# Mamba-2 scan and hard-swish MLP on one core: chunk 1's scan begun earlier within block 0's second product, weight parts cut into tiles of their own, and C and B of later chunks turned within the first product

## The chip, the cores and the metric

The kernel runs on one core of a Trainium2 chip. The metric is the device time of one execution in microseconds (us). Before the change, three runs gave 363.67, 364.67 and 365.08 us; their median, 364.67 us, is the time to compare with. The engines are named as in the profile: PE (matmuls), DVE (vector engine), ACT (scalar engine), POOL (GpSimd), SP (the queue that issues most DMAs).

## The reference, cut to what matters

```python
# scan: x (4, 8, 768, 32), a (4, 8, 768), B and C (4, 8, 768, 16)
for c in range(nc):
    cum = np.cumsum(la, axis=-1)                                   # la = log a of the chunk
    M = np.einsum('bhin,bhjn->bhij', Cc, Bc) * exp(cum_i - cum_j) * causal
    y = M @ xc + np.einsum('bhin,bhnd->bhid', Cc, state) * exp(cum)
    state = exp(sum la) * state + sum_j exp(cum_end - cum_j) * Bc_j xc_j
# (batch, head, seq, 32) -> 3072 rows of 256
h = x @ w_in                                                       # 256 x 2048
g = h * np.clip(h + 3.0, 0.0, 6.0) / 6.0
out = g @ w_out                                                    # 2048 x 256
```

## The kernel before, in words

**Blocks.** The 768 positions are cut into 6 chunks of 128. Chunk c gives, over 4 batches, 512 rows of 256 features, and these are block c of the MLP. Block k is computed in two products: the first (x @ w_in, with the hard-swish) in 16 units f of 128 features each, and the second (g @ w_out). The scan of chunk c = k + 1 runs within block k's second product, and its decays are loaded and made one chunk further ahead (`ahead` = k + 2).

**The scan of a chunk.** `turn` (or `turn_all`) turns B and C: bT, cT and csT, the last multiplied by the decay from the start, eto. `wake` makes the exponent of eto (ACT), `carry` (tmp, POOL) and `ends` (bs, POOL). `scores` is PE work: the old state into y (L501), the scores cb (L528), the new state's sums (L540). `multiply` multiplies the decays L by cb on DVE (L569), after `take`, a copy (adds) on ACT; `renew` makes the next state on DVE. `results` is `mix` (PE, L595 and L501), `keep` (four copies into yT on ACT, L610) and `split_y`, which cuts yT into three parts yh, yk and yl, so that the first product can run in a faster number type. `conceal` (POOL, L159) hides the upper triangle of the decays of the chunk ahead, and `decay_ends` makes their exponents, 8 on ACT (L386) and one product on POOL (L397) for each of 4 batches.

**The weights' parts.** In block 0 the first product uses w_in as it is. For the blocks after it, `in_weight_parts(i)`, i = 0 to 3, makes of each quarter of w_in the cut wh (ACT, L666, written over w_in itself), the remainder wl (POOL, L658) and a third part wk (DVE, L661). Before, two cuts of 128x512 (DVE, L640) go through a tile with two buffers, and the pieces of the four quarters are issued one after the other at units 1 to 8 of block 0's second product (`first_out`, 16 units of 8 PE entries).

**The first product of blocks 1 to 5.** `first(k, f + 2)` (yk by wk), `rest(k, f)` (yh by wh and yl by wl), then `seed` (scales what `first` made, in PSUM; before on ACT for odd f (L702) and on DVE for even f (L704)), `ramp` (ACT, L718) and `times_ramp` (DVE, L723; its output is gT(f)). rest(f) needs seed(f), which was issued two units before. `lead` issues `first` and `seed` of units 0 and 1 near the end of the block before. After every fourth unit `g_sums` puts three sums of 128x512 on POOL (L785).

**The second product of blocks 1 to 4** is `wide_units` (PE, L872), in 15 steps i; the scan's parts are called at given i. It needs four sums of parts of w_out, made on DVE by `weight_sums` (L764).

**What sets the order.** All engines run their instructions in the order in which the program issues them, and this is written out by hand in the loops at the end. An instruction that waits holds up all that stands behind it on its engine.

Of the kernel before, what the change touches and what calls it, by code (L numbers as in the profile page):

```python
# [8 lines left out]
FP32 = mybir.dt.float32  # L9
FP32R = mybir.dt.float32r  # L10
U32 = mybir.dt.uint32
# [10 lines left out]
def kernel(  # L22
# [427 lines left out]
    def turn(c, j):  # L450
        if j:
            turn_b(c)
        else:
            t_ps = turn_ps(c, 0)
            turn_c(c, t_ps)
            fade_c(c, t_ps)

    def wake(c):
        from_start(c)
        carry(c)  # L460
        for b in range(NB):
            ends(c, b)

    def turn_squares(t, out):

        nc.vector.transpose(
            out=out.rearrange("r b (s a) -> r b a s", a=4),
            in_=t.rearrange("s t b a n -> s (b a) t n"))

    def part_heads(c):  # L470
        _, cT, csT = turned(c)
        for t in range(2):
            nc.vector.tensor_scalar(
                out=cT[:, :, t], in0=csT, scalar1=parity[:, t:t + 1], scalar2=None,
                op0=ALU.mult)

    def fade(c, sl=slice(0, P), engine=nc.vector):
        csT = turned(c)[2][:, :, sl]
        engine.tensor_tensor(out=csT, in0=csT, in1=etos[c][:, :, sl], op=ALU.mult)

    def turn_all(c):
        bT, _, csT = turned(c)
        for t, out_ in zip(bcs[c], (csT, bT)):
            turn_squares(t, out_)
        part_heads(c)
        fade(c)

    def busy(n, bank):

# [144 lines left out]
    cuts, y_parts, banks = {}, {}, {}  # L634
    wl, wk, wh = {}, {}, {}

    def cut(src):

        t = att.tile([P, TB], U32, name="cut")
        nc.vector.tensor_scalar(  # L640
            out=t, in0=src.bitcast(U32), scalar1=0xFFFFF000, scalar2=None, op0=ALU.bitwise_and)
        return t.bitcast(FP32)

    def in_weight_parts(i):

        w = w_in[i]
        if i < 2:
            l, k = (const.tile([P, NK, TB], FP32R, name=f"w{n}{i}") for n in "lk")
        elif i == 2:
            both = loads.tile([P, 2, NK, TB], FP32R, name="wlk", tag="raw", bufs=NRAW)  # L650
            l, k = both[:, 0], both[:, 1]
        else:
            l, k = ([att.tile([P, TB], FP32R, name=n, tag=n) for _ in range(NK)]
                    for n in ("ws", "we"))
        wl[i], wk[i] = ([t[:, j] if i < 3 else t[j] for j in range(NK)] for t in (l, k))
        cuts[i] = [cut(w[:, j]) for j in range(NK)]
        for j in range(NK):
            nc.gpsimd.tensor_tensor(out=wl[i][j], in0=w[:, j], in1=cuts[i][j], op=ALU.subtract)  # L658
        yield
        for j in range(NK):  # L660
            nc.vector.scalar_tensor_tensor(  # L661
                out=wk[i][j], in0=wl[i][j].bitcast(FP32), scalar=-1.0 / FINE, in1=cuts[i][j],
                op0=ALU.mult, op1=ALU.add)
        h = const.tile([P, NK, TB], FP32R, name="wh", tag=f"w{i}")
        for j in range(NK):
            nc.scalar.copy(out=h[:, j], in_=cuts[i][j])  # L666
        wh[i] = [h[:, j] for j in range(NK)]
        yield

    def split_y(k):  # L670
        h, l, m = (att.tile([P, NK, TB], FP32R, name=f"y{n}", bufs=1) for n in "hlk")
        y_parts[k] = h, l, m
        for j in range(NK):
            y = yTs[k][:, j].rearrange("p b i -> p (b i)")
            t = cut(y)
            nc.scalar.copy(out=h[:, j], in_=t)
            nc.vector.scalar_tensor_tensor(  # L677
                out=m[:, j], in0=t, scalar=1.0 + FINE, in1=y, op0=ALU.mult, op1=ALU.subtract)
            nc.vector.scalar_tensor_tensor(
                out=l[:, j], in0=m[:, j].bitcast(FP32), scalar=-1.0 / FINE, in1=t,  # L680
                op0=ALU.mult, op1=ALU.add)

    def product(k, f, w, y, start=False):
        for j in range(NK):
# [13 lines left out]

    def seed(k, f):
        h = banks[k, f]  # L700
        if f % 2:
            nc.scalar.activation(h, h, AF.Copy, scale=-1.0 / (1.0 + FINE))  # L702
        else:
            nc.vector.tensor_scalar(  # L704
                out=h, in0=h, scalar1=-1.0 / (1.0 + FINE), scalar2=None, op0=ALU.mult)
# [240 lines left out]
        load_decay(c)  # L946
        load_eto(c)

    def results(c, parts=range(2)):
        mix(c, parts)  # L950
        keep(c)
        split_y(c)

# [75 lines left out]
    for k in range(NC):  # L1029
        gTs[k] = ffn.tile([P, NF, TB], FP32, name="gT")  # L1030
        c, ahead = k + 1, k + 2
        if k == 0:
            for f in range(NF):
                mlp_in(k, f)
                for i in weave.get(f, []):
                    weights(i, 1)
                if f in (6, 8):
                    diff_exp(c, f // 2 - 3)
            load(ahead)
            weights(NP + 1, 1)  # L1040
            weights(NP + 3, 1)
            weights(NP + 2, 3)
            sums = weight_sums()
            parts_in = [in_weight_parts(i) for i in range(NP)]
            for i in range(NP):
                for b in range(NB):
                    first_out(b, i, c)
                    if (i, b) == (0, 0):
                        weights(NP + 3, 1)
                        weights(NP + 2, 1)  # L1050
                        weights(NP + 3, 3)
                        rows(ahead)
                    elif 4 * i + b < 9:
                        next(parts_in[(4 * i + b - 1) // 2])
                    if (i, b) == (2, 0):
                        turn(c, 1)
                        wake(c)
                        turn(c, 0)
                        for p in range(2):
                            conceal(ahead, p)  # L1060
                    elif (i, b) == (2, 3):
                        scores(c)
                        multiply(c)
                        renew(c)
                        decay_ends(ahead, 0)
                        decay_ends(ahead, 1)
                        next(sums)
                    elif (i, b) == (3, 0):
                        next(sums)
                        decay_ends(ahead, 2)  # L1070
                    elif (i, b) == (3, 1):
                        results(c)
                        next(sums)
                        decay_ends(ahead, 3)
                    elif (i, b) == (3, 3):
                        from_start(ahead)
            rows(ahead + 1)
            continue
        for f in range(NF):
            if f == 0:  # L1080
                if ahead < NC:
                    load(ahead)
                if c < NC:
                    carry(c)
            if f + 2 < NF:
                first(k, f + 2)
            rest(k, f)
            if f + 2 < NF:
                seed(k, f + 2)
            ramp(k, f, banks[k, f])  # L1090
            times_ramp(k, f, banks[k, f])
            if f in (3, 7) and ahead < NC:
                conceal(ahead, f // 4)
            if f in (7, 11) and c < TURN:
                turn(c, f // 8)
            if f % 4 == 3:
                g_sums(k, f // 2 - 1)
        for i, _ in enumerate((wide_units if c < NC else out_units)(k)):
            if i == 0 and k == 1:
                next(sums)  # L1100
            if c < NC:
                if i == 1 and c == NC - 1:
                    own_banks(c)
                if i == 2:
                    scores(c)
                    multiply(c)
                    if c < NC - 1:
                        renew(c)
                if ahead < NC and 2 <= i < 6:
                    decay_ends(ahead, i - 2)  # L1110
                if i == 6 and c == TURN:
                    mix(c, (0,))
                if i == (7 if c == TURN else 6):
                    results(c, (1,) if c == TURN else range(2))
                    if ahead < NC:
                        from_start(ahead)
                    if ahead + 1 < NC:
                        rows(ahead + 1)
                if i == 9 and TURN <= ahead < NC:
                    turn_all(ahead)  # L1120
                if i == 5:
                    for j0 in range(0, NJ, 2):
                        last_sum(k, j0)
                if i == 12:
                    lead(c)

# [29 lines left out]
```

## Time and profile before

| What | Value |
|---|---|
| Median of 3 runs | 364.67 us (363.67 to 365.08) |
| The profiled execution | 363.47 us, its span 361.7 us |
| PE busy | 334.8 us, 93% of the span |
| DVE, ACT, POOL busy | 228.4 us (63%), 179.0 us (49%), 148.6 us (41%) |
| PE's share in the chain that ended last | 68% |

The span runs from the first to the last instruction of the profiled execution; 1.8 us of its time lie outside it. A row of the timeline gives start and duration in us, the engine, the line, what is written from what, the shapes, the number of instructions, and in brackets the idle time of the engine before them with what ended it. Where several instructions share a row, the duration is that of all of them. In block 0 the second product's matmuls run on plain fp32 and each shows as two PE entries. The first products lie at about 102 to 124, 154 to 176, 207 to 228, 258 to 280 and 312 to 333 us.

### The profile page before, as it was taken

Reading aid. Unit: us, or ns where it says so; the run is one execution under the profiler, and the core shown is the slowest. Engines: PE = TensorE matmul, PEld = TensorE weight load, DVE = VectorE, ACT = ScalarE, POOL = GpSimd, SP = SyncE. Lnnn points to the kernel's source line nnn. Section 1 sums busy time; section 2 is a strip of 40 time slices with the busy share of each in tenths; the row PEclk is TensorE's granted clock in tenths of the full one; section 3 lists DMA queues with packets and bytes.
Section 4 is the critical chain, followed back from the end, with each engine's and each line's share of the span. In section 5 each row is a group of like instructions: output and inputs, shape, how many; then the busy total and the mean of one; then the engine's idle time right before and its main releaser. Section 6 shows DMA issues by size and latency. Waiting matters only on the chain.

```text
span 361.7 us, 8315 instructions
## 1 busy us (share of the span) xinstructions
PE 334.8 (93%) x3408; PEld 268.1 (74%) x3408; DVE 228.4 (63%) x364; ACT 179.0 (49%) x372; POOL 148.6 (41%) x147
## 2 busy tenths in 40 slices
PE   6699999906899999999999999999999989999996
PEld 2454468805677888878888788888888868888996
DVE  6689999774768743976444967348876413576011
ACT  4677886134876646256374166293267012266000
POOL 3300000557118956419816338716048450069600
PEclk9999999965999999999999999999999999999999
DMA  8999989400057603425604325600110001110000
GB/s 164 187 304 163 230 206 139 96 0 2 31 143 85 94 5 73 90 31 60 97 4 98 69 35 65 88 4 2 30 30 2 2 2 16 24 22 1 2 29 29
DMA packets 91606, 24.90 MB, mean 69 GB/s; under 512 B 84208, under 2 KB 87952, under 8 KB 91056
## 3 DMA queue, kind: packets, MB, share of 16 engines
q1 hardware_dynamic: 87184, 23.06, 34.9%
q10 hardware_dynamic: 4384, 1.31, 1.7%
q8 instruction: 26, 0.43, 0.5%
q14 instruction: 12, 0.10, 0.1%
HBM read 21.07 MB, written 3.29 MB: 67 GB/s over the span
## 4 chain that ended last, share of the span: by engine, by line
PE 68%; DVE 15%; ACT 6%; DMA 4%; POOL 3%; issue 3%; SPq 1%; DVEq 0%; POOLq 0%; ACTq 0%
PE h L685 29%; PE wb L872 10%; PE wc L872 7%; PE wa L872 7%; PE oa L808 3%; PE ob L808 3%; DVE gT L723 2%; PE cb L528 2%; PE y L595 2%; DVE wm L206 2%; PE y L501 2%; DMA eto<-cum_e 2%; DMA raw<-in_moe_w_in_dram 2%; ACT L L386 2%; ACT we L222 2%
## 5 line engine op out<-in xcount | busy, mean ns | idle before, releaser
L718 ACT ACTIVATE gT<-h,half 128x512 f32<-128x512 f32 x96 | 65.9, 687 | 45.4 <-PE h L685 43.5
L723 DVE SCALAR_TENSOR_TENSOR gT<-gT,h 128x512 f32<-128x512 f32 x96 | 65.8, 687 | 33.8 <-ACT gT L718 32.6
L785 POOL TENSOR_TENSOR s<-gT 128x512 f32<-128x512 f32 x20 | 26.7, 1336 | 66.6 <-DVE gT L723 66.6
L685 PE MATMUL h<-yh,wh 128*128 128x512 f32 x160 | 50.3, 396 | 1.2 <-DVE h L704 1.2
L685 PEld LDWEIGHTS h<-yh,wh 128*128 128x128 f32 x160 | 29.6, 188 | 9.6 <-DVE h L704 2.3
L702 ACT ACTIVATE h<-h 128x512 f32<-128x512 f32 x40 | 23.5, 587 | 19.4 <-PE h L685 19.4
L386 ACT ACTIVATE L<-L,cum_n 128x64 f32<-128x64 f32 x128 | 31.4, 338 | 0.0
L569 DVE TENSOR_TENSOR L<-L,cb 128x512 f32<-128x512 f32 x24 | 15.3, 682 | 21.8 <-PE cb L528 18.2
L737 PE MATMUL o<-w_out,gT 128*128 128x256 f32 x128 | 28.8, 381 | 0.0
L704 DVE TENSOR_SCALAR h<-h 128x512 f32<-128x512 f32 x40 | 27.5, 689 | 0.6 <-PE h L685 0.6
L620 PE MATMUL h<-yT,w_in 128*128 128x512 f32 x64 | 27.7, 594 | 0.0
L685 PE MATMUL h<-yk,wk 128*128 128x512 f32 x80 | 26.2, 416 | 1.4 <-DVE yk L677 1.4
L737 PEld LDWEIGHTS o<-w_out,gT 128*128 128x128 f32 x128 | 24.2, 191 | 3.9 <-issue 0.6
L397 POOL TENSOR_TENSOR bs<-B,L 128x128 f32<-128x128 f32 x24 | 9.7, 413 | 41.4 <-ACT L L386 30.5
L785 POOL TENSOR_TENSOR s<-s,gT 128x512 f32<-128x512 f32 x20 | 25.7, 1287 | 1.6
L658 POOL TENSOR_TENSOR wl<-w_in,cut 128x512 fp32r<-128x512 f32 x4 | 5.2, 1324 | 50.1 <-DVE cut L640 50.1
L785 POOL TENSOR_TENSOR gT<-gT 128x512 f32<-128x512 f32 x20 | 25.7, 1283 | 0.0
L685 PE MATMUL h<-yl,wl 128*128 128x512 f32 x80 | 25.0, 394 | 0.0
L792 POOL TENSOR_TENSOR gT<-gT,s 128x512 f32<-128x512 f32 x16 | 21.2, 1359 | 5.0 <-PE wc L872 5.0
L620 PEld LDWEIGHTS h<-yT,w_in 128*128 128x128 f32 x64 | 12.1, 190 | 14.9 <-issue 12.9
L159 POOL TENSOR_SCALAR_AFFINE_SELECT L<-L 64x1024 f32<-64x1024 f32 (+1 forms) x16 | 18.3, 1146 | 7.9 <-DMA L<-cum_d 7.5
L685 PEld LDWEIGHTS h<-yk,wk 128*128 128x128 f32 x80 | 15.0, 188 | 5.2 <-DVE yk L677 1.5
(156 smaller groups left out, 635.1 us busy)
## 6 DMA issues: line engine op xcount, KB each, us to landing
raw<-in_moe_w_out_dram SPq DMA_DIRECT2D x4, 1024.0 KB
L<-cum_d SPq DMA_DIRECT2D x8, 512.0 KB
xt<-in_x_dram SPq DMA_DIRECT2D x6, 512.0 KB
raw<-in_moe_w_in_dram SPq DMA_DIRECT2D x3, 1024.0 KB
out_dram<-back SPq DMA_DIRECT2D x128, 16.0 KB
eto<-cum_e SPq DMA_DIRECT2D x20, 64.0 KB
B<-in_B_dram SPq DMA_DIRECT2D x5, 256.0 KB
raw<-in_moe_w_in_dram ACTq DMA_DIRECT2D x1, 1024.0 KB
```

The source lines that it names most:

```text
L386: nc.scalar.activation(Ls[c][:, b, h], Ls[c][:, b, h], AF.Exp, bias=cum_n[:, c, g:g + 1])
L620: nc.tensor.matmul(out=h.rearrange("p r i -> p (r i)"), lhsT=w_in[f // FP][:, j, f % FP * P:(f % FP + 1) * P], rhs=yTs[k][:, j].rearrange( ...
L685: nc.tensor.matmul(out=banks[k, f].rearrange("p r i -> p (r i)"), lhsT=w[f // FP][j][:, f % FP * P:(f % FP + 1) * P], rhs=y[:, j], start=( ...
L702: nc.scalar.activation(h, h, AF.Copy, scale=-1.0 / (1.0 + FINE))
L704: nc.vector.tensor_scalar(out=h, in0=h, scalar1=-1.0 / (1.0 + FINE), scalar2=None, op0=ALU.mult)
L718: nc.scalar.activation(gTs[k][:, f], h.rearrange("p r i -> p (r i)"), AF.Relu, bias=half, scale=1.0 / 6.0)
L723: nc.vector.scalar_tensor_tensor(out=g, in0=g, scalar=1.0, in1=h.rearrange("p r i -> p (r i)"), op0=ALU.min, op1=ALU.mult)
L737: nc.tensor.matmul(out=o[:, b % 2], lhsT=gTs[0][:, f, b * P:(b + 1) * P], rhs=w_out[:, f], start=(f == 0 and b % 2 == 0), stop=True, skip_ ...
L785: nc.gpsimd.tensor_tensor(out=o, in0=p_, in1=q_, op=op)
L792: nc.gpsimd.tensor_tensor(out=gsums[k][4][:, js], in0=g_quarter(k, 1, 0)[:, js], in1=gsums[k][2][:, js], op=ALU.subtract)
L808: nc.tensor.matmul(out=bank[:, slot], lhsT=lhs[:, j], rhs=rhs[:, j], start=(clear and j == 0), stop=True, skip_group_check=True)
L872: nc.tensor.matmul(out=bank[:, slot], lhsT=lhs[:, j], rhs=rhs[:, j], start=(clear and j == 0), stop=True, skip_group_check=True)
```

## The change

- `cut` makes one tile of 128x1024 instead of two of 128x512, with one buffer, for the weights as for yT. The four weight cuts get tiles that are unused at that time (those of yh, yl and two output tiles), and each quarter is now issued in three pieces: cut; wl with wh; wk.
- `split_y` works on 128x1024 in four instructions instead of eight.
- In block 0's second product the pieces are issued at other units: B and C of chunk 1 are turned after unit 7 instead of 8, its scores come after unit 9 instead of 11, its results after unit 11 instead of 13. The weights' pieces stand between these steps.
- The four sums of w_out move from block 0's second product, and the start of block 1's, to units 1, 5, 9 and 13 of block 1's first product.
- `seed` is on DVE for every fourth unit only, else on ACT.
- For chunks 3 to 5 `turn_all` is no longer at step 9 of a second product, but in four pieces after units 2, 5, 8 and 11 of the first product of blocks 2 to 4.
- `results` is no longer split in two for chunk 3.

```diff
     def turn_all(c):
         bT, _, csT = turned(c)
-        for t, out_ in zip(bcs[c], (csT, bT)):
-            turn_squares(t, out_)
+        turn_squares(bcs[c][0], csT)
+        yield
+        turn_squares(bcs[c][1], bT)
+        yield
         part_heads(c)
+        yield
         fade(c)
+        yield
...
-    def cut(src):
-
-        t = att.tile([P, TB], U32, name="cut")
+    def cut(src, pool=att, tag="cut"):
+
+        t = pool.tile([P, NK, TB], U32, name="cut", tag=tag, bufs=1)
...
-        w = w_in[i]
+        t = cuts[i] = cut(
+            w_in[i], *((att, "yh"), (att, "yl"), (ffn, "wide"), (ffn, "back"))[i])
+        yield
...
-        cuts[i] = [cut(w[:, j]) for j in range(NK)]
         for j in range(NK):
-            nc.gpsimd.tensor_tensor(out=wl[i][j], in0=w[:, j], in1=cuts[i][j], op=ALU.subtract)
+            nc.gpsimd.tensor_tensor(
+                out=wl[i][j], in0=w_in[i][:, j], in1=t[:, j], op=ALU.subtract)
+        h = const.tile([P, NK, TB], FP32R, name="wh", tag=f"w{i}")
+        nc.scalar.copy(out=h, in_=t)
+        wh[i] = [h[:, j] for j in range(NK)]
         yield
         for j in range(NK):
             nc.vector.scalar_tensor_tensor(
-                out=wk[i][j], in0=wl[i][j].bitcast(FP32), scalar=-1.0 / FINE, in1=cuts[i][j],
+                out=wk[i][j], in0=wl[i][j].bitcast(FP32), scalar=-1.0 / FINE, in1=t[:, j],
                 op0=ALU.mult, op1=ALU.add)
-        h = const.tile([P, NK, TB], FP32R, name="wh", tag=f"w{i}")
-        for j in range(NK):
-            nc.scalar.copy(out=h[:, j], in_=cuts[i][j])
-        wh[i] = [h[:, j] for j in range(NK)]
         yield
...
     def seed(k, f):
         h = banks[k, f]
-        if f % 2:
+        if f % 4:
...
-                    elif 4 * i + b < 9:
-                        next(parts_in[(4 * i + b - 1) // 2])
-                    if (i, b) == (2, 0):
+                    elif (i, b) == (1, 3):
                         turn(c, 1)
                         wake(c)
+                        part(0)
                         turn(c, 0)
+                        part(1, 0)
+                    elif (i, b) == (2, 1):
+                        scores(c)
+                        part(1)
+                        multiply(c)
+                        renew(c)
+                        part(2, 2)
                         for p in range(2):
                             conceal(ahead, p)
+                        part(3, 3)
+                        decay_ends(ahead, 0)
                     elif (i, b) == (2, 3):
-                        scores(c)
-                        multiply(c)
-                        renew(c)
-                        decay_ends(ahead, 0)
+                        part(0, 1)
+                        results(c)
                         decay_ends(ahead, 1)
-                        next(sums)
                     elif (i, b) == (3, 0):
-                        next(sums)
+                        part(2, 3)
+                    elif (i, b) == (3, 1):
                         decay_ends(ahead, 2)
-                    elif (i, b) == (3, 1):
-                        results(c)
-                        next(sums)
                         decay_ends(ahead, 3)
...
+            if k == 1 and f % 4 == 1:
+                next(sums)
...
+            if f in (2, 5, 8, 11) and TURN <= c < NC:
+                if f == 2:
+                    turning = turn_all(c)
+                next(turning)
...
-            if i == 0 and k == 1:
-                next(sums)
...
-                if i == 6 and c == TURN:
-                    mix(c, (0,))
-                if i == (7 if c == TURN else 6):
-                    results(c, (1,) if c == TURN else range(2))
+                if i == 6:
+                    results(c)
...
-                if i == 9 and TURN <= ahead < NC:
-                    turn_all(ahead)
```

More of the change, by code (lines that the diff above doesn't have):

```diff
@@ L654, in in_weight_parts @@
                     for n in ("ws", "we"))
-        wl[i], wk[i] = ([t[:, j] if i < 3 else t[j] for j in range(NK)] for t in (l, k))
-        cuts[i] = [cut(w[:, j]) for j in range(NK)]
+        wl[i], wk[i] = ([x_[:, j] if i < 3 else x_[j] for j in range(NK)] for x_ in (l, k))
         for j in range(NK):
-            nc.gpsimd.tensor_tensor(out=wl[i][j], in0=w[:, j], in1=cuts[i][j], op=ALU.subtract)
+            nc.gpsimd.tensor_tensor(
[3 more added lines that the diff above has]
+        wh[i] = [h[:, j] for j in range(NK)]
         yield
@@ L672, in split_y @@
         y_parts[k] = h, l, m
[L673 to L681, printed above, removed]
+        y = yTs[k].rearrange("p j b i -> p j (b i)")
+        t = cut(y)
+        nc.vector.scalar_tensor_tensor(
+            out=m, in0=t, scalar=1.0 + FINE, in1=y, op0=ALU.mult, op1=ALU.subtract)
+        nc.scalar.copy(out=h, in_=t)
+        nc.vector.scalar_tensor_tensor(
+            out=l, in0=m.bitcast(FP32), scalar=-1.0 / FINE, in1=t, op0=ALU.mult, op1=ALU.add)
     def product(k, f, w, y, start=False):
@@ L947, in rows, with results @@
         load_eto(c)
-    def results(c, parts=range(2)):
-        mix(c, parts)
+    def results(c):
+        mix(c)
         keep(c)
@@ L1044, with part @@
             parts_in = [in_weight_parts(i) for i in range(NP)]
+            def part(*pieces):
+                for i_ in pieces:
+                    next(parts_in[i_])
             for i in range(NP):
@@ L1110 @@
                     decay_ends(ahead, i - 2)
-                if i == 6 and c == TURN:
-                    mix(c, (0,))
-                if i == (7 if c == TURN else 6):
-                    results(c, (1,) if c == TURN else range(2))
+                if i == 5:
+                    for j0 in range(0, NJ, 2):
+                        last_sum(k, j0)
+                if i == 6:
+                    results(c)
                     if ahead < NC:
@@ L1118 @@
                         rows(ahead + 1)
-                if i == 9 and TURN <= ahead < NC:
-                    turn_all(ahead)
-                if i == 5:
-                    for j0 in range(0, NJ, 2):
-                        last_sum(k, j0)
                 if i == 12:
```

## The prediction

> **What bounds the kernel now.** I read the waits of PE first, then the timeline around the longest. (Us in total, times, longest.)
>
> ```profile
> PE y L501 <- DVE csT L448: 12.5, 1, 12.5
> PE h L685 <- DVE yk L677: 1.4, 2, 1.2
> PE h L685 <- DVE h L704: 1.2, 3, 0.5
> ```
>
> PE is busy 93% of the span, so an edit pays only where PE idles, and it idles above all once: 12.5 us before chunk 1's scan, in block 0. The third row (0.28, 0.40 and 0.53 us) is all that the seeds cost today. What fills the hole, from the timeline:
>
> ```profile
> 65.05 0.76 DVE L640 TENSOR_SCALAR cut<-w_in 128x512 uint32<-128x512 uint32 x2
> 65.55 2.61 POOL L658 TENSOR_TENSOR wl<-w_in,cut 128x512 fp32r<-128x512 f32 x2 [48.52 <-DVE cut L640]
> ...
> 66.97 2.35 DVE L661 SCALAR_TENSOR_TENSOR wk<-wl,cut 128x512 fp32r<-128x512 f32 x2 [1.16 <-POOL wl L658]
> 68.19 1.14 ACT L666 CAST wh<-cut 128x512 fp32r<-128x512 f32 x2 [6.62 <-POOL wl L658]
> ...
> 80.69 1.14 ACT L666 CAST wh<-cut 128x512 fp32r<-128x512 f32 x2 [3.02 <-POOL ws L658]
> 81.73 0.58 ACT L432 COPY bT<-t_ps 128x512 f32<-128x512 f32 x1
> ```
>
> Each quarter of w_in goes DVE, POOL, DVE and ACT in 4.17 us (65.05 to 69.24), four times in turn, and the scan's copies stand behind the last on ACT. Further down, before block 1:
>
> ```profile
> 84.97 4.67 POOL L159 TENSOR_SCALAR_AFFINE_SELECT L<-L 64x1024 f32<-64x1024 f32 x4
> ...
> 89.06 5.84 ACT L386 ACTIVATE L<-L,cum_n 128x64 f32<-128x64 f32 x24
> ...
> 95.26 1.19 ACT L610 ACTIVATE yT<-y 128x256 f32<-128x256 f32 x4
> ...
> 101.77 0.71 PE L685 MATMUL h<-yh,wh 128*128 128x512 f32 x2 [0.28 <-DVE h L704]
> ```
>
> 24 of 32 decays come before yT, and rest(0) of block 1 starts at 101.77. From there a unit takes 1.39 us; rest(4) starts at 107.40.
>
> The last view is what POOL does to DVE:
>
> ```profile
> 140.31 5.58 POOL L792 TENSOR_TENSOR gT<-gT,s 128x512 f32<-128x512 f32 x4
> ```
>
> ```profile
> 141.65 1.42 DVE L640 TENSOR_SCALAR cut<-yT 128x512 uint32<-128x512 uint32 x1 [3.26 <-ACT yT L610]
> 143.11 1.65 DVE L677 SCALAR_TENSOR_TENSOR yk<-cut,yT 128x512 fp32r<-128x512 f32 x1
> 144.79 1.64 DVE L679 SCALAR_TENSOR_TENSOR yl<-yk,cut 128x512 fp32r<-128x512 f32 x1
> 146.35 0.41 DVE L640 TENSOR_SCALAR cut<-yT 128x512 uint32<-128x512 uint32 x1
> ```
>
> With POOL busy, DVE instructions from SBUF alone take about 1 us longer (0.41 becomes 1.42, 0.69 becomes 1.65). Those that read PSUM do not: gT by L723 takes 0.69 beside POOL.
>
> **Part 1: block 0's second product.** Instructions of 128x1024 are priced by rows of that size, from start to start: a cut 0.60 (L202), yk or yl 1.15 (L237), wh 1.14 (the two halves above); a wk of 128x512 by L677, 0.6. A unit is 8 PE entries of 0.2225 us (24 in 5.34), 1.78. B is turned one unit earlier, at 66.09 - 1.78 = 64.3. ACT: bT 64.9, eto done 66.0. POOL: tmp and bs take 2.05 (82.92 to 84.97), to 68.1; wl of quarters 0 and 1, 5.2, to 73.3. By then PE has done the scores (two units from 65.2, then 2.4): 71.1, where before it did them until 88.7. So the 12.5 us go. But what is late next is not on PE. ACT's order is now wh0, wh1, adds, wh2, wh3, 8 decays, yT, and each wh waits for its wl, since it overwrites w_in. wh1 ends at 73.3 + 1.14 = 74.45, adds 74.8, the state on DVE 75.45; only behind it stands the cut of quarter 2: 76.05. POOL idles until then and does wl2, the four conceals and wl3: 2.6 + 4.67 + 2.6 = 9.87. Four wk of quarters 0 and 1 come in between on DVE. What one costs POOL: the four L792 above took 5.58 instead of 4.94 with two DVE instructions let in, 0.3 each; so 1.2, wl3 ends at 87.15. ACT: wh3 1.14, decays 8 x 0.243 = 1.95, yT 0.95 (95.26 to 96.21): yT at **R = 91.2**, 5.0 earlier than before.
>
> The Trainium skill, "SBUF — State Buffer", section "Who interferes with whom", says that DVE and GpSimd share a port pair as an exclusive lock, held for the whole instruction. Read so, a wk would cost POOL its whole 0.60 to 0.69, not the row's 0.3, and R would be 92.4. I take the row.
>
> Much of the 5.0 is given back, because now 24 decays stand behind yT on ACT. From R: yh to +1.8, 8 decays +3.75, the copy of o waits for wk2 on DVE (cut 0.6, yk 1.15, yl 1.15, wk2 1.2) and ends +4.85, 16 decays +8.75, seed(1) +9.3, second copy +9.8, eto +10.35, seed(2), now on ACT, +10.95, ramp(0) +11.6, seed(3) +12.2, ramp(1) +12.85. DVE: gT(1) +13.5, the first sum of w_out (1.21 in its row, 1.15 from start to start) +14.65, seed(4) +15.3. So rest(4) starts at 91.2 + 15.35 = 106.55, against 107.40: **-0.85**. Bounds: R from 90.0 (POOL loses nothing) to 92.4 (it loses a whole wk, 0.6, each of four times), so -2.05 to +0.35. DVE's wk3 and seed(0) end at +6.0 and are covered by ACT. The clock: it fell to 0.50 in the hole and was back at 1.00 after 3.8 us of work (84.8 to 88.5); now PE idles from 82.9 to about 93, and then has 4.5 us of work (three `first` at half speed and four entries) before rest(0), so I price it at nothing; uncovered, a unit at half clock costs 1.4.
>
> **Part 2: the w_out sums in block 1's first product.** Before, they stood partly ahead of the first seeds (99.80 to 100.93) and of nothing at 125.8. Now a DVE wait there reaches PE. rest(f) has gT(f) done 2.53 after it starts (101.77 to 104.3), and a seed issued behind gT(f) for f + 3 has 4.17 - 2.53 = 1.64 us. The second sum (1.15) and seed(8) (0.65) need 1.8 and have 1.64 + 0.35, as PE stops for transposes at unit 7 (112.49 to 112.84): no stall if POOL is idle, up to 1.0 behind a conceal (1.15). I take 0.45, since POOL's conceals start as their loads land, about then. The third sum comes behind cT and csT of unit 7 (2.0 us, 114.07 to 116.08), gT(8) and gT(9), with POOL in its sums without a pause. After rest(7) starts, that is 2.53 + 2.0 + 2 x 0.6 + 1.15 + 0.65 = 7.53 against 5 x 1.39 + 0.35 = 7.30, and DVE is then some 0.3 behind from the second sum: seed(12) is late by 0.55 with no block, by 1.8 with a whole one (1.25); I take the middle, 1.2. The fourth has no seed behind it. The 0.40 at unit 10 goes, as that seed is on ACT. Sum: +0.45 + 1.2 - 0.4 = **+1.25** (+0.15 to +2.4).
>
> **Part 3: turning in the first products of blocks 2 to 4.** The two transposes (1.1 each; beside POOL's conceals at 148.7 to 151.0 they took 1.11 and 1.13) fit: bT behind gT(5) leaves seed(8) just in time (1.0 + 0.65 against 1.64). cT after unit 8 decides. Block 2's rows now:
>
> ```profile
> 167.74 0.69 DVE L723 SCALAR_TENSOR_TENSOR gT<-gT,h 128x512 f32<-128x512 f32 x1
> 169.19 0.69 DVE L723 SCALAR_TENSOR_TENSOR gT<-gT,h 128x512 f32<-128x512 f32 x1 [0.76 <-ACT gT L718]
> ```
>
> ```profile
> 167.88 1.29 POOL L785 TENSOR_TENSOR s<-gT 128x512 f32<-128x512 f32 x1
> 169.25 1.29 POOL L785 TENSOR_TENSOR s<-s,gT 128x512 f32<-128x512 f32 x1
> 170.50 1.29 POOL L785 TENSOR_TENSOR gT<-gT 128x512 f32<-128x512 f32 x1
> ```
>
> gT(8) frees DVE at 168.37; rest(12) starts at 171.44. Unblocked, the two cT (0.4 each), gT(9) and seed(12) end in time. Blocked once, the first cT ends at 169.6 and seed(12) at 171.3: in time. Blocked twice, the second ends at 171.2, gT(9) 171.8, seed(12) 172.4: rest(12) 1.05 late. The three blocked rows above each wait for their predecessor; the two cT do not, so either can be. I take 0.55, three times 1.65 (0 to 3.9 with 1.3 each). The 0.53 us before block 3 go, since DVE's turning (200.54 to 204.8) stood ahead of that seed: **+1.1** (-0.5 to +3.4). The loads of C and B on SP now wait for these transposes; behind them only x is queued until the next second product, some 15 us later: nothing.
>
> **Part 4, at nothing:** the merged split_y has over 3 us before `lead` in blocks 1 to 4; four ramps of 0.69 and three seeds of 0.59 keep ACT busy 4.5 of 5.56 us per four units; the undivided results run as in the other blocks. Without such cover each costs about what a late seed costs today, 0.5. The 2.0 us that PE loses once in block 4 with no releaser are not touched.
>
> **Sum:** -0.85 + 1.25 + 1.1 = +1.5. The profiled execution took 363.47 (span 361.7 and 1.8 around it), so 365.0 by its own measure. It lies 1.2 below the runs' median, so I forecast 364.67 + 1.5 = **366.2 us**. About 0.5% (1.8 us) is what a measurement of this kernel can tell from no change.
>
> **Rivals.** *Faster, POOL and DVE seldom meet:* R = 90.0, sums unblocked, cT blocked at most once: -2.05 + 0.15 - 0.5 = -2.4, **362.3**. For it: both POOL and DVE have pauses. It decides at wl3's end, below 86. Chance 0.20. *The hole is simply filled,* 12.5 us less, **352**: against it stands ACT's order; 0.03. *Slower, they meet each time:* R = 92.4, each sum and both cT behind a POOL instruction: +0.35 + 2.4 + 3.4 = +6.2, **370.9**. For it: POOL runs without pause at just these units. It decides where the second cT starts behind a new POOL instruction. Chance 0.25. The forecast has 0.52, from 364.3 to 368.1, of which 0.27 lie within 0.5%. So faster 0.23, same 0.27, slower 0.50. The range takes in both of these, near enough (the filled hole stays outside): 361.5 to 371.
>
> **What would show it.** Right: no wait of PE at L501 of 12 us, but one of some 10 us at `first`, on yk; wh3 near 88 and yT near 91; rest(4) near 106.5; waits of `rest` on DVE seeds at units 4, 8 and 12 of block 1 and 12 of blocks 2 to 4. Wrong: yT before 88, or block 2's first product as long as before (21.4 us).

## The result and the profile after

The changed kernel takes 366.0 us (median of 20 runs, 364.0 to 372.0), the kernel before 363.26 us (20 runs, 362.7 to 365.1). The ratio is 1.0066, with a 95% interval of 1.0048 to 1.0085: about 2.4 us slower. The ratios leave disturbed runs out, the medians hold all runs. The profiled execution took 367.65 us, its span 365.7 us.

PE's waits after the change (us in total, times, longest):

```profile
PE h L688 <- DVE yk L680: 11.0, 1, 11.0
PE h L688 <- DVE h L707: 3.6, 5, 1.1
...
PE h L688 <- ACT h L705: 0.7, 1, 0.7
```

The 12.5 us before the scan (L501 for csT) are gone, and 11.0 us have come at `first`, which waits for yk. The second row is five stops for a seed on DVE (1.2 us in three before). Where the 11 us are made, from the rows of POOL, ACT, DVE and PE in block 0's second product:

```profile
76.87 3.32 POOL L663 TENSOR_TENSOR wlk<-w_in,cut 128x512 fp32r<-128x512 f32 x2 [2.68 <-DVE cut L644]
80.15 5.92 POOL L159 TENSOR_SCALAR_AFFINE_SELECT L<-L 64x1024 f32<-64x1024 f32 x4
86.03 2.48 POOL L663 TENSOR_TENSOR ws<-w_in,cut 128x512 fp32r<-128x512 f32 x2
```

```profile
88.55 1.04 ACT L666 CAST wh<-cut 128x1024 fp32r<-128x1024 f32 x1 [7.28 <-POOL ws L663]
89.50 2.01 ACT L386 ACTIVATE L<-L,cum_n 128x64 f32<-128x64 f32 x8
91.42 1.16 ACT L614 ACTIVATE yT<-y 128x256 f32<-128x256 f32 x4
...
97.62 3.93 ACT L386 ACTIVATE L<-L,cum_n 128x64 f32<-128x64 f32 x16
```

```profile
76.11 1.29 DVE L644 TENSOR_SCALAR cut<-w_in 128x1024 uint32<-128x1024 uint32 x2
77.31 6.53 DVE L670 SCALAR_TENSOR_TENSOR wk<-wl,cut 128x512 fp32r<-128x512 f32 x4
92.61 0.69 DVE L644 TENSOR_SCALAR cut<-yT 128x1024 uint32<-128x1024 uint32 x1 [8.77 <-ACT yT L614]
...
105.88 1.22 DVE L767 TENSOR_TENSOR t<-w_out 128x1024 f32<-128x1024 f32 x1
107.02 0.69 DVE L707 TENSOR_SCALAR h<-h 128x512 f32<-128x512 f32 x1
```

```profile
107.76 0.73 PE L688 MATMUL h<-yh,wh 128*128 128x512 f32 x2 [1.12 <-DVE h L707]
...
114.39 0.73 PE L688 MATMUL h<-yh,wh 128*128 128x512 f32 x2 [0.36 <-DVE h L707]
```

Read from the end: `rest(4)` (107.76) waits for the seed of 107.02, that for the w_out sum of 105.88; and the whole stage for yT, which ACT writes at 91.42, behind wh3 (88.55), behind the last wl (86.03), behind four conceals that took 5.92 us (4.67 before). The decays of 97.62 hold up ACT's first seed as well. In blocks 2 to 4, here block 2:

```profile
168.94 2.64 DVE L473 TENSOR_SCALAR cT<-csT,parity 128x512 f32<-128x512 f32 x2
171.50 0.68 DVE L726 SCALAR_TENSOR_TENSOR gT<-gT,h 128x512 f32<-128x512 f32 x1
172.10 0.69 DVE L707 TENSOR_SCALAR h<-h 128x512 f32<-128x512 f32 x1
```

```profile
172.84 0.74 PE L688 MATMUL h<-yh,wh 128*128 128x512 f32 x2 [0.63 <-DVE h L707]
```

Two instructions that fill cT take 2.64 us beside POOL's sums, and `rest(12)` stops behind the seed of 172.10. The same happens at 225.05 (0.49) and 277.79 (1.04).

A ledger by stages, from the start of the second product's wa in each block (us from the span's start; the last column is oa of block 5):

| Kernel | block 1 | block 2 | block 3 | block 4 | block 5 |
|---|---|---|---|---|---|
| before | 124.21 | 175.61 | 228.03 | 279.40 | 333.31 |
| changed | 124.69 | 177.11 | 229.30 | 282.03 | 337.25 |
| difference | +0.48 | +1.50 | +1.27 | +2.63 | +3.94 |

Of these differences 0.52 us lie ahead of anything that the change touches: block 0's second product starts at 51.07 us here and at 50.55 before, and the clock of the changed execution had stood at 0.50 from 15.1 to 18.5 us, where that of before stood at 1.00. So the change itself costs 0.0, 1.0, 0.8 and 2.1 us up to blocks 1, 2, 3 and 4. The interval of the ratio comes to 1.7 to 3.1 us, and 2.1 lies in it. The last 1.31 us belong to this execution again: after a stop of PE in block 4 the clock was 0.50 from 301.8 to 305.2 us, a mean of 0.68 over 300 to 305. The rows of the windows view (window, its length, busy us and instructions of PE, PEld, DVE, ACT and POOL, then clock, DMA share, GB/s) of before and of the changed kernel:

```profile
300.00:305.00 5.00, 5.00 (x25) 4.41 (x24) 1.83 (x4) 0.89 (x2) 0.00 (x0) 1.00 0.12 18
```

```profile
300.00:305.00 5.00, 4.09 (x14) 3.27 (x14) 3.24 (x4) 1.43 (x2) 0.00 (x0) 0.68 0.01 3
```

### The profile page after: what moved, and what is told of

Its sections match the earlier page's. It is cut to its first block, busy times and chain, and to the rows that moved or that the text cites. A ratio compares the mean times of both kernels' runs of the same rounds, so it can differ in the third digit from the quotient of the medians.

```text
span 365.7 us, 8306 instructions
## 1 busy us (share of the span) xinstructions
PE 338.7 (93%) x3408; PEld 270.1 (74%) x3408; DVE 218.4 (60%) x325; ACT 188.1 (51%) x383; POOL 160.4 (44%) x147
## 3 DMA queue, kind: packets, MB, share of 16 engines
q10 hardware_dynamic: 4384, 1.31, 1.6%
## 4 chain that ended last, share of the span: by engine, by line
PE 66%; issue 13%; DVE 8%; POOL 4%; DMA 4%; ACT 4%; SPq 1%; POOLq 0%; DVEq 0%; ACTq 0%
PE h L688 24%; PE wb L875 12%; PE wc L875 8%; PE wa L875 8%; PE oa L811 3%; PE ob L811 3%; DVE cT L473 2%; PE y L599 2%; PE y L505 2%; PE cb L532 2%; DMA raw<-in_moe_w_in_dram 2%; DMA eto<-cum_e 1%; DVE gT L726 1%; POOL L L159 1%; POOL wl L663 1%
## 5 line engine op out<-in xcount | busy, mean ns | idle before, releaser
L726 DVE SCALAR_TENSOR_TENSOR gT<-gT,h 128x512 f32<-128x512 f32 x96 | 64.6, 683 | 34.3 <-ACT gT L721 33.3
L788 POOL TENSOR_TENSOR s<-gT 128x512 f32<-128x512 f32 x20 | 28.8, 1440 | 70.7 <-DVE gT L726 59.4
L688 PE MATMUL h<-yh,wh 128*128 128x512 f32 x160 | 51.5, 403 | 4.3 <-DVE h L707 3.6
L705 ACT ACTIVATE h<-h 128x512 f32<-128x512 f32 x60 | 35.3, 588 | 29.7 <-PE h L688 29.7
L688 PE MATMUL h<-yk,wk 128*128 128x512 f32 x80 | 27.4, 435 | 11.0 <-DVE yk L680 11.0
L404 POOL TENSOR_TENSOR tmp<-state,eto 128x256 f32<-128x256 f32 x5 | 6.1, 1210 | 50.9 <-ACT eto L390 50.9
L397 POOL TENSOR_TENSOR bs<-B,L 128x128 f32<-128x128 f32 x24 | 10.2, 436 | 40.6 <-ACT L L386 29.8
L688 PEld LDWEIGHTS h<-yk,wk 128*128 128x128 f32 x80 | 15.8, 198 | 14.7 <-ACT yh L682 11.4
L795 POOL TENSOR_TENSOR gT<-gT,s 128x512 f32<-128x512 f32 x16 | 24.1, 1539 | 5.0 <-PE wc L875 5.0
L159 POOL TENSOR_SCALAR_AFFINE_SELECT L<-L 64x1024 f32<-64x1024 f32 (+1 forms) x16 | 20.5, 1285 | 7.1 <-PE h L688 5.2
L644 DVE TENSOR_SCALAR cut<-yT 128x1024 uint32<-128x1024 uint32 x5 | 5.8, 1155 | 24.9 <-ACT yT L614 24.9
```

The costliest lines, as they stand in the source:

```text
L159: nc.gpsimd.affine_select(out=t[rows], in_=t[rows], pattern=pattern, compare_op=ALU.is_ge, fill=-1e5, base=base, channel_multiplier=-1)
L688: nc.tensor.matmul(out=banks[k, f].rearrange("p r i -> p (r i)"), lhsT=w[f // FP][j][:, f % FP * P:(f % FP + 1) * P], rhs=y[:, j], start=( ...
L726: nc.vector.scalar_tensor_tensor(out=g, in0=g, scalar=1.0, in1=h.rearrange("p r i -> p (r i)"), op0=ALU.min, op1=ALU.mult)
L788: nc.gpsimd.tensor_tensor(out=o, in0=p_, in1=q_, op=op)
L795: nc.gpsimd.tensor_tensor(out=gsums[k][4][:, js], in0=g_quarter(k, 1, 0)[:, js], in1=gsums[k][2][:, js], op=ALU.subtract)
```

## The experiments

Ten kernels, each in five rounds beside the kernel before. The theory: the change loses at the seeds on DVE, since w_out's sums and cT stand ahead of them there, and it gains nothing in block 0, since yT still stands behind POOL's and ACT's work. Rivals: DVE's load as such; the lock between POOL and DVE; ACT's work as such.

| Kernel | Median, us | Ratio to before, 95% interval |
|---|---|---|
| e1_turn_later | 362.83 | 0.9979 (0.9948 to 1.0009) |
| e2_sums_later | 364.19 | 1.0018 (0.9989 to 1.0047) |
| f1_both_later | 360.40 | 0.9927 (0.9892 to 0.9962) |
| e3_pool_quiet | 366.15 | 1.0073 (1.0040 to 1.0106) |
| f2_pool_quiet | 362.73 | 0.9990 (0.9955 to 1.0024) |
| f3_seed_even | 367.07 | 1.0091 (1.0055 to 1.0128) |
| h1_stage_alone | 363.96 | 1.0012 (0.9976 to 1.0048) |
| e4_yt_first | 364.64 | 1.0019 (0.9990 to 1.0049) |
| g1_stage | 351.58 | 0.9685 (0.9637 to 0.9734) |
| g2_stage | 352.83 | 0.9685 (0.9642 to 0.9729) |

**Turning moved by one unit.**

```diff
-            if f in (2, 5, 8, 11) and TURN <= c < NC:
+            if f in (2, 6, 10, 13) and TURN <= c < NC:
```

> The changed kernel with one edit: the four turning pieces of blocks 2 to 4 stand after units 2, 6, 10 and 13 instead of 2, 5, 8 and 11, so that no DVE seed follows the two cT. Theory A (the late seed(12) is the price of turning: PE waited 0.63, 0.49 and 1.04 us for it): the three waits go, 2.1 us less than the changed kernel (366.0), so about 0.6 us above the kernel before. Rival B (DVE has simply too much to do in a first product, the place does not matter): the waits move to other units and the time stays.

Measured: 0.9979, so some 3.2 us (0.87%) better than the changed kernel. All three stops at rest(12) are gone, and the steps from block to block fall from 52.42, 52.19 and 52.73 to 51.41, 51.25 and 51.27 us. Issued behind the DVE seed of that window instead of ahead of it, the same work costs nothing. The new place also meets POOL less often, here in block 2:

```profile
172.40 1.59 DVE L473 TENSOR_SCALAR cT<-csT,parity 128x512 f32<-128x512 f32 x2
```

In blocks 2 to 4 the pair takes 1.59, 1.47 and 0.88 us, against 2.64, 2.50 and 3.04 in the changed kernel. So e1 alone does not separate the place from the wait for POOL.

**Sums of w_out moved by one unit.**

```diff
-            if k == 1 and f % 4 == 1:
+            if k == 1 and f in (2, 6, 10, 13):
```

> The changed kernel with one edit: the four sums of w_out stand after units 2, 6, 10 and 13 of block 1's first product instead of 1, 5, 9 and 13, behind the DVE seeds instead of ahead of them. Theory A (a sum ahead of seed(4) and seed(8) is what PE waited for, 1.12 and 0.36 us): both waits go, and about 1.0 to 1.5 us of the time. Rival B (seed(4) is late because ACT runs its ramps late after the 16 decays, the sum adds nothing): the wait at unit 4 stays at about 1 us and the time is that of the changed kernel.

Measured: the stops of 1.12 and 0.36 us in block 1 are gone, wa of block 1 starts at 122.33 instead of 124.69 (0.55 us of that lie ahead of the edit, as block 0's second product starts at 50.52 instead of 51.07), and the ratio is 1.0018, some 1.7 us better than the changed kernel. Rival B, which kept the wait at unit 4, is out.

**Both moves.**

> The changed kernel with both moves at once: the running sums of w_out in block 1's first product come after units 2, 6, 10 and 13, and the turning of C and B in blocks 2 to 4 too, instead of after units 3, 7, 11 and 14. If the costs of the two parts are the stalls at the rest of units 4, 8 and 12 and nothing else (my theory), the two gains add: 366.0 less 2.1 (three stalls of 0.63, 0.49 and 1.04 us) less 1.4 (1.12 and 0.36 us, less what stays of them), 362 to 363 us, about 1 us below the kernel before. If the stalls only hide that DVE, ACT or POOL is what paces these stretches (the rival), the second move gives nothing on top of the first: 363 to 364 us.

Measured: 360.40 us, below the 362 to 363 that the theory expected: by the ratios some 5 us (1.4%) better than the changed kernel. No row for a DVE seed is left among PE's waits:

```profile
PE h L688 <- DVE yk L680: 11.0, 1, 11.0
...
PE h L688 <- ACT h L705: 0.7, 1, 0.7
```

The traces say why the sum of the idle times (3.6 us) was too small. Block by block this kernel needs 51.30, 51.25 and 51.26 us, 1.12, 0.94 and 1.47 less than the changed one, whose idle times shown there are 0.63, 0.49 and 1.04. In block 2 the matmul pairs start 0.46 us apart and are shown 0.62 long; around the stop of 0.63 the starts are 1.26 apart (171.58 to 172.84) and the next 0.58: 0.92 us lost. The other 0.2 us are a late start at unit 8, with no idle time shown at all (starts 0.56 apart instead of 0.46 and 0.57 after it). Together 1.13.

**Is it the lock?** First the issue of POOL's sums was moved:

```diff
-            if f % 4 == 3:
+            if f % 4 == 3 and not (quiet and f == 7):
+                if quiet and f == 11:
+                    g_sums(k, 2)
                 g_sums(k, f // 2 - 1)
```

(`quiet` is 1 < k < 5; the conceal of unit 7 is moved in the same way.)

> The changed kernel with POOL kept free around the two cT: in blocks 2 to 4 the sums and the conceal that follow unit 7 are issued after unit 11, ahead of that unit's own. DVE's instructions and their places are unchanged. Theory A (POOL and DVE block each other): the two cT take 0.8 us instead of 2.6, the three waits for seed(12) go, 2.1 us less than the changed kernel, unless POOL's later sums hold up the second product. Rival B (DVE is late by its own load): the cT take as long, and the waits stay.

This did not test the lock. Nothing else lies on POOL between the two places, and POOL starts as soon as its data is there, so its sums still ran from 167.65 us (168.56 in the changed kernel, where all of block 2 lies 0.9 us later) and cT still took 2.62 us; the time stayed (1.0073). A later place in the program is not a later start. So the sums were made to need later data, by joining those of units 4 to 7 with those of units 8 to 11:

```diff
-    def g_sums(k, j0):
+    def g_sums(k, j0, n=2):
...
-        js = slice(j0, j0 + 2)
+        js = slice(j0, j0 + n)
...
-            if f % 4 == 3:
+            if f % 4 == 3 and 1 < k < 5 and f in (7, 11):
+                if f == 11:
+                    g_sums(k, 2, 4)
+            elif f % 4 == 3:
```

> The changed kernel, but in blocks 2 to 4 POOL's running sums of units 4 to 7 and of units 8 to 11 are one instruction each instead of two, so that they wait for the data of unit 11 and POOL does nothing while the quarter cT is turned. If the pair that fills cT is long (2.5 to 3.0 us) because POOL's sums run beside it (lock theory), it takes 0.8 us, the waits at the rest of unit 12 (0.63, 0.49 and 1.04 us) go, and the time falls by about 2 us to 364 us. If DVE is late at unit 12 from the load of the turning itself (rival), pair and waits stay and the time is that of the changed kernel, 366 us. A later sum could hold up the second product: that would show as a wait of PE for POOL there, and as more than 366 us.

DVE's row in block 2, and the next instruction of POOL's sums:

```profile
168.78 0.88 DVE L473 TENSOR_SCALAR cT<-csT,parity 128x512 f32<-128x512 f32 x2
```

```profile
173.17 2.79 POOL L788 TENSOR_TENSOR s<-gT 128x1024 f32<-128x1024 f32 x1 [4.68 <-DVE gT L726]
```

With POOL idle the pair takes 0.88 us instead of 2.64, the three stops are gone, and the ratio is 0.9990, some 2.8 us better than the changed kernel. The lock theory holds: DVE was not late from the load of the turning, but from waiting for POOL. There are two cures for one stall: take away the block, or put the blocked work where nobody waits. The second shows in f1, where one of the two cT is still blocked in block 2 (1.56 us for the pair), and nobody waits.

**The seeds as they were.**

```diff
-        if f % 4:
+        if f % 2:
```

> The changed kernel with the seeds of chunk 1 divided between DVE and ACT as before the change (every even unit on DVE) instead of every fourth on DVE. The prediction put this at nothing. By it: 365.5 to 366.5 us, with the waits of PE for a seed on DVE at units 4, 8 and 12 as they are. If DVE's load in the first products is what makes these seeds late (rival), three more seeds of 0.4 to 0.7 us a block add to the waits: 367 to 369 us.

The median lies in the rival's interval, but the traces do not show it there: the blocks take 52.34, 52.24 and 52.84 us against 52.42, 52.19 and 52.73, and DVE seeds stop PE five times for 3.3 us against 3.6. The intervals of the two ratios overlap. I read this as nothing, and leave open whether half a microsecond is hidden in it.

**The first part of the change alone.** The sums and the turning go back to where they were before the change.

> Part 1 alone: the changed kernel with the sums of w_out back in block 0's second product and at the start of block 1's, and with the turning of C and B for chunks 3 to 5 back at step 9 of a second product, as before the change. The prediction gave this part -0.85 us. By it PE's wait for csT stays away, the waits at unit 4 of block 1 and at unit 12 of blocks 2 to 4 go, the old late seed ahead of block 3 (0.53 us) comes back, and the time is 362 to 363 us, some 1 us under the kernel before. If the earlier scan gains nothing on its own (rival), it is that of the kernel before, 363.5 us; if the sums in block 0 hold up yk on DVE, it is 364 us or more.

Measured: 1.0012, no difference that can be told, so the theory's 1 us was wrong here. The median lies between the rival's 363.5 us and the third case's 364, and the trace shows a wait of the third kind, though at the seed and not at yk. PE's waits:

```profile
PE h L688 <- DVE yk L680: 11.0, 1, 11.0
PE h L688 <- DVE h L707: 3.4, 1, 3.4
```

The second is rest(0), which waits for the very first seed until 102.37 us (before: 101.77). DVE's rows tell whose it is:

```profile
95.38 1.22 DVE L767 TENSOR_TENSOR t<-w_out 128x1024 f32<-128x1024 f32 x1
96.51 1.50 DVE L670 SCALAR_TENSOR_TENSOR wlk<-wlk,cut 128x512 fp32r<-128x512 f32 x2
97.94 1.28 DVE L670 SCALAR_TENSOR_TENSOR we<-ws,cut 128x512 fp32r<-128x512 f32 x2
99.14 1.21 DVE L767 TENSOR_TENSOR t<-t,w_out 128x1024 f32<-128x1024 f32 x1
100.39 1.22 DVE L767 TENSOR_TENSOR t<-w_out,t 128x1024 f32<-128x1024 f32 x1
101.53 0.69 DVE L707 TENSOR_SCALAR h<-h 128x512 f32<-128x512 f32 x1
```

Three sums stand between yl and the seed. Counted from the start of block 0's second product (50.55 us before, 50.72 here, 50.39 in f1), wa of block 1 comes after 73.66 us before, 75.00 here and 71.84 in f1. So the parts are not independent: with the earlier scan, the sums cost time in block 0 (here) and ahead of the seeds of block 1 (73.62 us in the changed kernel), and none that shows behind those seeds (f1). What the sums' move would give the kernel before, without the earlier scan, no run shows.

**The 11 us, first attempt.** wl3 as before, but wh3 and the first eight decays behind yT on ACT.

```diff
                 out=wl[i][j], in0=w_in[i][:, j], in1=t[:, j], op=ALU.subtract)
+        if i == 3:
+            yield
...
-                        decay_ends(ahead, 0)
...
                         results(c)
+                        part(3)
+                        decay_ends(ahead, 0)
                         decay_ends(ahead, 1)
```

> The changed kernel with ACT's order alone changed before block 1: the last weight cut wh3 and the first 8 decays stand behind yT and yh instead of ahead of them. POOL's order is the same. Theory A (yT was late because it stood on ACT behind wh3, which waits for POOL's last wl): yT comes some 10 us earlier, at about 82 instead of 92.6, PE's wait of 11.0 us for yk shrinks to about 3, but seed(1) still stands behind 32 decays and wh3 on ACT, so rest(1) gains only about 3 us, and so the time (363). Rival B (yT was late because of DVE's and POOL's chain, not ACT's order): yT and the time stay where they were.

yT comes at 80.61 instead of 91.42 and PE waits 3.9 us for yk instead of 11.0, as expected, but by the ratios only some 1.7 us are left of it, less than the 3 expected. The wait has moved:

```profile
PE h L690 <- DVE yk L682: 3.9, 1, 3.9
PE h L690 <- ACT h L707: 3.7, 1, 3.7
...
PE h L690 <- ACT L L386: 1.7, 1, 1.7
```

32 decays now stand in one piece between yh and the first seed on ACT (91.22 to 99.34), and from 93.35 to 102.7 PE's pairs last 1.05 to 1.22 us instead of 0.62: the granted clock is 0.50 from 86 to 102 us. That the stops keep it there is inferred.

**The 11 us, the whole order.** g1 rounds all four quarters early (two of the cuts in buffers of loads that are free), brings the conceals forward on POOL, makes the exponent of the next eto earlier, spreads the 32 decays over ACT's pauses, makes the last quarter's parts in block 1's first product, and has the two moves of f1. In block 0's second product:

```diff
                     elif (i, b) == (1, 3):
...
-                        part(1, 0)
+                        part(1, 2, 3)
+                        conceal(ahead, 0)
+                        from_start(ahead)
                     elif (i, b) == (2, 1):
                         scores(c)
-                        part(1)
                         multiply(c)
+                        decay(ahead, 0)
+                        part(0)
                         renew(c)
-                        part(2, 2)
-                        for p in range(2):
-                            conceal(ahead, p)
-                        part(3, 3)
-                        decay_ends(ahead, 0)
+                        conceal(ahead, 1)
+                        decay(ahead, 1)
                     elif (i, b) == (2, 3):
-                        part(0, 1)
-                        results(c)
-                        decay_ends(ahead, 1)
+                        part(0)
+                        mix(c)
+                        keep(c)
+                        decay(ahead, 2)
+                        part(1, 1)
+                        split_y(c)
+                        part(2)
+                        decay(ahead, 3)
...
```

> Another order of the same work in block 0's second product: all four parts of W_in are rounded and yT is made before ACT's run of decays, the decays of chunk 1 are spread over ACT's idle time, the last two parts of the weights come in block 1's first product, and the sums of w_out and the turning are moved as in the two kernels before. If the 11 us that PE waits for yk is ACT's and DVE's order of work (my theory: yT stands behind wh3 and eight decays on ACT, wk3 ahead of the cut on DVE), PE goes on at about 84 to 86 us instead of 94.7, rest(4) of block 1 comes 12 to 15 us earlier, the clock is not halved there, and the time is 350 to 354 us. If ACT's whole work in the stage is what bounds it (rival, as the gain of only 1.4 us hints when yT was put first), the wait comes back as PE waiting for seeds or for the decays and the time is 361 to 364 us.

Measured: 351.58 us, 0.9685, a time as the theory had it. ACT's rows of the same stage:

```profile
78.65 1.05 ACT L666 CAST wh<-cut 128x1024 fp32r<-128x1024 f32 x1 [0.75 <-POOL wl L663]
79.60 2.02 ACT L386 ACTIVATE L<-L,cum_n 128x64 f32<-128x64 f32 x8
81.52 1.16 ACT L614 ACTIVATE yT<-y 128x256 f32<-128x256 f32 x4
```

yT is written right after PE has made it, PE's wait for yk is 3.1 us, and `rest(4)` of block 1 starts at 101.33, 4.6 us ahead of f1 (105.94), although this profiled execution had lost time early: its clock stood at 0.50 from 20 to 28 us, and the scores that start at 69.30 us in the changed kernel start 3.8 us later here, at 73.09. The median, 351.6 us, is below its 354.98. Against the changed kernel `rest(4)` comes 6.4 us earlier, 10.2 when both are counted from the start of block 0's second product (54.85 here), and not 12 to 15; and the clock was still 0.50 from 91.4 to 94.8 us. So it was order in the main, and not ACT's whole work; as g1 moves work on ACT, DVE and POOL at once, the share of each is not shown.

**The last 3 us.** In g2 `split_y` stands ahead of the second quarter's third parts on DVE (and of its cut wh on ACT), and the last quarter's third part comes after unit 3.

> The rearranged stage of the last kernel, with two things moved on DVE: the cut of yT with yk and yl stands ahead of the third weight parts of the second quarter, and the third part of the last quarter comes after unit 3 of block 1's first product instead of unit 1. If PE's last wait of 3.1 us is that order (my theory: yT was done at 82.7 us, and its cut started at 88.2, behind four third parts that took 5.9 us), the cut starts by 85 us, the wait falls under 1 us, the 1.1 us at the rest of unit 4 goes as well, and the time is 347 to 349 us against 351.6. If the third parts are needed as soon as yk is (rival: first needs both), the wait stays between 2 and 3 us and the time is 350 to 352 us.

Measured: 352.83 us, 0.9685 again; the theory's gain did not come. This profiled execution took 357.95 us, 5 us above the median, so its waits are a hint at most. The wait for yk fell to 1.4 us, but:

```profile
PE h L688 <- DVE h L707: 2.8, 3, 2.1
...
PE h L688 <- DVE yk L680: 1.4, 1, 1.4
...
PE h L688 <- DVE gT L726: 1.2, 1, 1.2
```

The seeds of unit 0 now stand behind four third parts (2.1 us), and the part moved to unit 3 met POOL (3.31 us for two) and held up gT. DVE is busy 10.93 of the 11 us from 82 to 93 there, so a new order may only choose who waits; that this is what bounds the ordinary executions is not shown.

## Why the prediction came out as it did

The side was right, and the time almost exactly: 366.2 forecast, 366.0 measured. That closeness is luck. The forecast was a rise of 1.5 us on top of a median of three runs, 364.67; over twenty runs before has 363.26, and the rise is 2.4 to 2.7 us. The rise in turn is a sum whose parts were off by 0.7 to 1.1 us, not all the same way. By steps:

- **The hole is not filled: right.** The 12.5 us became 11.0 at yk, by the chain that was named: POOL's remainders and conceals, wh3, eight decays, yT. e4 and g1 show that chain by taking it apart.
- **R, yT's end, was 91.2 and came at 92.6.** Of these 1.4 us, 0.5 lie ahead of the change, in the late start of block 0's second product. The rest is POOL in the main. From 76.87 to 86.03 it took 9.16 us for work that needs 2.48 (the row of ws) and 4.67 (the conceals before the change) when nobody stands in its way: 2.0 us more, where the forecast had 1.2 for four third parts. A fifth DVE instruction falls into that time, the second cut in the row of 76.11, which the forecast did not count. That is 0.4 us each, not 0.3. Read by the rule of the Trainium skill, "SBUF — State Buffer", section "Who interferes with whom", each would have cost POOL its whole 0.60 to 0.69; the measured 0.4 lies between the two, nearer to the row that I took.
- **What follows R was right:** 15.35 us to rest(4) forecast, 107.76 - 92.6 = 15.2 measured. So part 1 is +0.36 by the two traces, -0.16 without the 0.52 that lie ahead of the change, instead of -0.85. The clock was back at 1.00 only at 100.4 us, after rest(0) had begun, but PE then waited 0.68 us for ACT's seed(1), so pricing it at nothing held.
- **Part 2 was too dear:** from rest(4) to block 1's wa the change costs 16.93 - 16.81 = +0.12 instead of +1.25. The second sum was blocked (1.96 us) and stopped PE by 0.36, near the 0.45 forecast. The third, which was to cost 1.2 us, took 1.21, was not blocked, and stopped nobody. DVE came first, and POOL waited instead:

```profile
118.56 1.21 DVE L767 TENSOR_TENSOR t<-w_out,t 128x1024 f32<-128x1024 f32 x1
```

```profile
117.46 3.32 POOL L159 TENSOR_SCALAR_AFFINE_SELECT L<-L 64x1024 f32<-64x1024 f32 x2
```

  The errors of parts 1 and 2, +0.7 and -1.1 us, nearly cancel: together 0.0 measured, +0.40 forecast.
- **Part 3 was too cheap:** +2.15 us by the ledger (2.63 - 0.48), +1.1 forecast; with it the rise is 2.1, not 1.5. Mechanism and place were right (two blocked cT, rest(12)), and the idle times, 0.63, 0.49 and 1.04, are near the 0.55 each. But a stop costs more than the idle time shown, 0.94 to 1.47 us a block, and unit 8, "just in time", was a little late.
- **Part 4 at nothing:** f3 does not contradict it for the seeds; the merged `split_y` and the undivided results were not run alone.
- **The rivals:** "they meet each time" had the right mechanism for cT, not for the sums.

What stays open is the clock in block 4. The mean of 0.68 after a stop of 1.60 us came in this profile (0.71 in that of e1, after 1.68 us) and not in that of before, which stopped for 1.98 us. One reading fits: the clock changes in steps of 3.41 us (below), and the stop lies whole within one such step in the changed kernel (298.4 to 301.8) and in e1 (296.1 to 299.5), while in before, counted on from its rise at 88.9 us, a step ends at 297.1, inside the stop (296.7 to 298.7). No run tests it.

## What to carry to other kernels

Work put on an engine that also feeds the bound engine on a schedule should be issued just behind such an instruction, not ahead of it: one unit's difference was worth 3.2 us here, about as much as removing the block itself (2.8). A wait that is removed uncovers the next in the same stage, so follow what the waiting value needs on every engine in turn, and move all of it, or little comes out (1.7 us in e4, some 14 in g1, which has the two moves of f1 too). Price a stall by the starts of the stalled instructions, not by the idle time shown.

## What the runs showed of the hardware

- Of POOL and DVE on SBUF, the one that comes first makes the other wait, and either can lose: cT took 2.64 us for two beside POOL's sums and 0.88 without; two conceals took 3.32 us (117.46) instead of 2.38 (166.22) beside a DVE sum that kept its 1.21.
- The granted clock changes in steps of 3.41 us: in the twelve traces its stretches at 0.50 last 3.41, 6.83, 13.65 or 17.07 us, but for one that the end of a trace cuts off, and the stretches at 1.00 between them are whole multiples of 3.41 too.
- So it comes back after a delay that varies. In f1 PE works without a pause from 94.02 us, and the clock is 0.53 from 96 to 100 us and 1.00 from 100 on, so some 5.7 us after the restart. In before PE restarts at 84.78 and the clock is 1.00 from 88.9, so 4.1 us (the prediction read 3.8). The Trainium skill, "TensorE: Matmul & The Clock Gate", Part 1, gives at least one window of some 3.4 us of work for the way up, at least one such window of idleness for the way down, and windows that run freely. The steps, and both 4.1 and 5.7, agree with that; the fall after a stop of 1.60 us does not, and here the measurement decides.
